# Two groups of attention matmuls a step instead of four in a fused attention and MoE kernel

## The chip, the core and the metric

The kernel runs on one core of a Trainium2 chip. The metric is the time of one execution in device microseconds: the median of three runs before the change is 851.68 us (850.89 to 852.7). Traces and pages come from one profiled execution. Engines are named as the profile names them: PE (TensorE) with its weight loads PEld, DVE (VectorE), ACT (ScalarE), POOL (GpSimd) and SP (SyncE, which issues all DMAs here; its queue is SPq).

## What is computed

Attention for 8 batches of 8 heads with 512 local and 32 global tokens of 64 values: global tokens attend to all, local tokens to the global ones and to a window of 32 to each side. Its output, 4608 tokens of 512 values, goes through a layer that takes the largest of three products and multiplies it by a fourth matrix.

```python
    s_g = scale * np.matmul(q_g, k_all.transpose(0, 1, 3, 2))
    out_g = np.matmul(sm(s_g), v_all)
    s_ll = scale * np.matmul(q_l, k_l.transpose(0, 1, 3, 2))
    mask = np.abs(pos[:, None] - pos[None, :]) <= window
    s_ll = np.where(mask, s_ll, -1000000000.0)
    s_lg = scale * np.matmul(q_l, k_g.transpose(0, 1, 3, 2))
    a_l = sm(np.concatenate([s_lg, s_ll], axis=-1))
    out_l = np.matmul(a_l, np.concatenate([v_g, v_l], axis=2))
...
    h = np.maximum(np.maximum(x @ w1, x @ w2), x @ w3)
    return (h @ w_out).astype(np.float32)
```

Everything is in 32-bit floats. From tile 28 on the attention's operands, and in the MoE layer all of them, are split in a high part and a rest, so that a product is made of two or three matmuls.

## The kernel before

**Tiles and steps.** Two heads make a pair `p`; a batch has four pairs, and a pair four tiles of 128 local queries. There are 128 tiles `sl`, with `t = sl % 4`. The main loop makes one step for each tile (lines 510 to 539). A step works on several tiles at once, since each is at another stage: it transposes the probabilities of tile `sl + 1` (`trans`, four matmuls into the PSUM tile `T`, read by a copy and, from tile 26 on, a subtraction into `pt`), computes the scores of tile `sl + 3` (`next_scores` calls `scores`; PSUM tile `S`), and multiplies tile `sl`'s probabilities with the values (`pv`, PSUM tile `O`). For the next pair's global tokens, `glob` makes scores in the steps with `t` 0 and 1 (PSUM tile `S` again) and `glob_soft` their softmax in the step with `t` 2; six small DMAs (line 298) bring it into `probg`. `transg` transposes one block of `probg` for tile `sl + 1` (one matmul, PSUM tile `S`), and its copy completes `pt`.

**The way of the local scores.** VectorE reads the score tile with the mask and finds the extreme value (line 325), ScalarE takes the exponential and its sum (line 327), VectorE the reciprocal (lines 329 and 330), some engine multiplies by it (`times`, mostly POOL at line 112), and SP issues the DMA into one of two `prob` tiles (line 334). Two steps later `trans` reads it.

**The MoE layer in the gaps.** From tile 16 on the previous batch's MoE layer runs between these pieces. `moe_group` is a generator that issues one wide matmul (512 columns) each time it is asked: 216 at line 425 (PSUM tile `pm`, three buffers) and 72 at line 444. `fill(n)` asks for `n`. A step asks for 4 + 4 + 3 + 7 = 18, so that 16 steps make the 288 of one batch. The last batch and the global tokens' MoE layer come after the loop.

**Buffers.** The tiles named `S` share two PSUM buffers, `T` and `O` have one each.

**Order.** TensorE keeps the program's order but for a few places. On all engines a scheduler in the framework orders the instructions when the program is built, and the functions `copy`, `sub` and `times` give work to the engine with the least load by their own planned costs; each engine then runs its own list in order and waits at its head.

**Weights.** Up to tile 25 the steps also convert the MoE weights (`weight_step`): a DMA into `wraw` (line 160), an absolute value on ScalarE (165), four bit operations on VectorE (168 to 171), a copy on ScalarE (178) and a subtraction on POOL (182).

## Time and profile before

| | before |
|---|---|
| median of three runs | 851.68 us (850.89 to 852.7) |
| the profiled execution | 852.36 us |
| its span, first to last instruction | 850.6 us |
| mean granted TensorE clock | 0.981 |
| first step of the changed kind (tile 16) begins | about 79 us |
| last attention matmul | about 744 us |

A line of the page names the source line, the engine, the operation and its tiles as out<-in; a timeline row has the start, the time from the first instruction's start to the last one's end, and the instructions that were merged (x4). The time of a busy matmul in such a row overlaps with the next one's, so that distances between starts are the better measure; the chain's pieces are made of these. A bracket is idle time of the engine ahead of the instruction, with what ended it. A row by stretches has the length, each engine's busy time with its instructions, the granted clock, the DMA share and GB/s.

### The profile page before, as it was taken

To read this page: it belongs to the slowest core of one execution; us is meant where nothing else is said; L and a number is where in the kernel's file an instruction comes from. 1 tells how busy PE (TensorE), PEld (TensorE's weight loads), DVE (VectorE), ACT (ScalarE), POOL (GpSimd) and SP (SyncE) were. 2 spreads that over 40 slices of the span, in tenths; PEclk is the share of its full clock that TensorE was granted. 3 is DMA by queue.
4 is the path that set the end of the run, shared out by engine and by line. 5 is a ranking of instruction groups with operands and counts; after the bars stand their busy time and mean duration, and the time that the engine had idled before them with its cause. 6 is when DMAs were issued, how large, how long until landed. Compare 5 with 4: busy or idle time off the path is not lost.

```text
span 850.6 us, 15712 instructions
## 1 busy us (share of the span) xinstructions
PE 811.6 (95%) x4452; PEld 674.6 (79%) x4452; DVE 566.0 (67%) x1784; ACT 527.9 (62%) x1479; POOL 510.0 (60%) x683
## 2 busy tenths in 40 slices
PE   6767987999999999999999999999999999999997
PEld 4545666788888888888888888888888888888896
DVE  4768786776777777777777777867786776421111
ACT  5666556767767676766776777776776676411111
POOL 5645666786668666766768766866676664411211
PEclk9798989999999999999999999999999999999999
DMA  6655755434333533353333433253335322100000
GB/s 199 173 175 159 223 168 161 125 109 136 111 108 89 155 101 104 105 163 113 95 107 114 136 110 102 85 161 106 98 113 162 101 85 67 65 12 1 25 25 25
DMA packets 102886, 95.12 MB, mean 112 GB/s; under 512 B 20752, under 2 KB 93584, under 8 KB 102800
## 3 DMA queue, kind: packets, MB, share of 16 engines
q1 hardware_dynamic: 102800, 94.12, 36.3%
q8 instruction: 36, 0.59, 0.3%
q14 instruction: 50, 0.41, 0.2%
HBM read 56.85 MB, written 8.91 MB: 77 GB/s over the span
## 4 chain that ended last, share of the span: by engine, by line
PE 87%; DVE 5%; DMA 2%; issue 2%; ACT 2%; SPq 1%; POOL 0%; DVEq 0%; ACTq 0%; POOLq 0%
PE pm L425 48%; PE pm L444 17%; PE O L394 7%; PE S L322 5%; PE T L346 4%; PE S L277 2%; PE O L387 1%; DVE wraw L170 1%; DMA wraw<-w_in 1%; PE S L367 1%; PE pm L318 1%; PE S L318 1%; DVE cut L169 1%; DVE cut L168 1%; PE S L273 0%
## 5 line engine op out<-in xcount | busy, mean ns | idle before, releaser
L425 PE MATMUL pm<-xs,wh 128*128 128x512 f32 (+1 forms) x1296 | 409.4, 389 | 0.8 <-POOL xs L94 0.8
L425 PEld LDWEIGHTS pm<-xs,wh 128*128 128x128 f32 x1296 | 234.2, 190 | 32.8 <-POOL xs L94 1.2
L425 PE MATMUL pm<-xs,wl 128*128 128x512 f32 (+1 forms) x648 | 254.1, 392 | 0.0
L112 POOL TENSOR_SCALAR s<-s,z 128x192 f32<-128x192 f32 (+1 forms) x220 | 101.6, 474 | 67.0 <-ACT lox L102 36.5
L425 PEld LDWEIGHTS pm<-xs,wl 128*128 128x128 f32 x648 | 123.0, 190 | 23.5 <-issue 2.4
L444 PE MATMUL pm<-woh,h 128*128 128x512 f32 x408 | 133.4, 398 | 0.0
L94 POOL TENSOR_TENSOR h<-m,h 128x512 fp32r<-128x512 f32 (+1 forms) x54 | 67.9, 1258 | 99.6 <-ACT h L102 99.6
L433 DVE TENSOR_TENSOR m<-pm,m 128x512 f32<-128x512 f32 (+1 forms) x108 | 71.2, 659 | 72.6 <-PE pm L425 71.6
L327 ACT ACTIVATE s<-s,nm 128x192 f32<-128x192 f32 (+1 forms) x224 | 103.1, 461 | 9.1 <-DVE nm L325 6.9
L94 POOL TENSOR_TENSOR qs<-qraw,qs 128x256 fp32r<-128x256 f32 x100 | 73.9, 749 | 57.4 <-ACT qs L102 44.0
L94 DVE TENSOR_TENSOR pt<-T,pt 128x512 fp32r<-128x512 f32 x102 | 70.5, 691 | 46.4 <-ACT pt L102 44.7
L329 DVE TENSOR_SCALAR z<-z 128x2 f32<-128x2 f32 x128 | 54.9, 429 | 48.7 <-ACT s L327 47.6
L444 PEld LDWEIGHTS pm<-woh,h 128*128 128x128 f32 x408 | 74.6, 188 | 11.6
L325 DVE CUSTOM_DVE_ANT_0 s<-S,mask 128x192 f32<-128x192 f32 (+1 forms) x224 | 74.7, 371 | 12.0 <-PE S L318 5.5
L444 PE MATMUL pm<-wol,h 128*128 128x512 f32 x204 | 81.7, 401 | 0.0
L94 POOL TENSOR_TENSOR vs<-vraw,vs 128x256 fp32r<-128x256 f32 x102 | 75.2, 737 | 7.7 <-ACT vs L102 3.6
L94 POOL TENSOR_TENSOR kst<-kraw,kst 64x576 fp32r<-64x576 f32 x49 | 70.1, 1430 | 11.4 <-issue 6.9
L102 ACT CAST pt<-T 128x512 fp32r<-128x512 f32 x90 | 52.7, 586 | 38.3 <-PE T L346 38.3
L102 ACT CAST qs<-qraw 128x256 fp32r<-128x256 f32 x100 | 40.7, 407 | 56.1 <-PE S L322 55.1
L394 PEld LDWEIGHTS O<-pt,vs 128*128 128x128 f32 x408 | 66.4, 188 | 9.2
L394 PE MATMUL O<-pt,vs 128*128 128x320 f32 (+1 forms) x408 | 72.8, 299 | 0.0
L346 PEld LDWEIGHTS T<-identr,prob 128*128 128x128 f32 x448 | 50.8, 141 | 20.6 <-ACT xr L102 2.3
(100 smaller groups left out, 1312.4 us busy)
## 6 DMA issues: line engine op xcount, KB each, us to landing
vraw<-v_in SPq DMA_DIRECT2D x128, 128.0 KB, 2.3
qraw<-q_in SPq DMA_DIRECT2D x100, 128.0 KB, 2.2
prob<-s SPq DMA_DIRECT2D x56, 224.0 KB, 2.4
prob<-s SPq DMA_DIRECT2D x56, 192.0 KB, 2.3
wraw<-w_in SPq DMA_DIRECT2D x18, 512.0 KB, 4.8
out_dram<-o SPq DMA_DIRECT2D x32, 256.0 KB, 2.5
kraw<-k_in SPq DMA_DIRECT2D x25, 320.0 KB, 3.1
qn<-q_in SPq DMA_DIRECT2D x28, 128.0 KB, 2.8
```

The source lines that it names most:

```text
L94: (dve if least(c) == "d" else pool).tensor_tensor(out=out, in0=a, in1=b, op=ALU.subtract)
L102: act.copy(out=out, in_=a)
L112: pool.tensor_scalar(out=out, in0=a, scalar1=col, scalar2=1.0, op0=ALU.mult, op1=ALU.mult)
L322: pe.matmul(ph[j][:, 0:n], lhsT=qs[sl][:, a, 128 * j:128 * j + 128], rhs=kst[p][:, j, c0:c0 + n], start=(a == 0), stop=(a == 1))
L325: dve.tensor_tensor_reduce(out=s[:, j, 0:n], in0=ph[j][:, 0:n], in1=mask[:, (1, 0, 1, 0)[t], 32 * (t == 0):32 * (t == 0) + n], scale=-0.12 ...
L327: act.activation(out=s[:, j, 0:n], in_=s[:, j, 0:n], func=AF.Exp, bias=nm[:, j:j + 1], scale=-1.0, accum_out=z[:, j:j + 1])
L329: dve.tensor_scalar(out=z, in0=z, scalar1=1e-9, scalar2=None, op0=ALU.add)
L346: i = pe.transpose(pr[:, 256 * j + 128 * c:256 * j + 128 * c + 128], s[:, j, 128 * c:128 * c + 128], one)
L394: pe.matmul(o[:, j, 0:320].rearrange("p (a q) -> p a q", a=2)[:, :, 0:n], lhsT=vs[sl][:, 2 * j + c].rearrange("p a d -> p (a d)"), rhs=pt[ ...
L425: pe.matmul(ps[:, 0:n], lhsT=w[f][:, i, k], rhs=xs[k][:, a, 0:n], start=(q == 0), stop=(q == 11))
L433: dve.tensor_tensor(out=m[:, 0:n], in0=ps[:, 0:n], in1=m[:, 0:n], op=ALU.max)
L444: pe.matmul(ps, lhsT=hh[f][:, a, 128 * t:128 * t + 128], rhs=w[:, f], start=(q == 0), stop=(q == 17))
```

## The change

```diff
@@ -514,21 +514,30 @@
+        steady = sl >= EARLY
         trans(sl + 1)
-        fill(4)
+        if not steady:
+            fill(4)
         next_scores(max(min(sl + 5, EARLY - 1), sl + 3))
         if t == 2:
             split_k(p + 2)
             load_k(p + 3)
-        fill(4)
+        if steady:
+            fill(8)
+            transg(sl + 1)
+        else:
+            fill(4)
         pv(sl)
         if t <= 1:
             glob(p + 1, t)
         elif t == 2:
             glob_soft(p + 1)
-        fill(3)
-        transg(sl + 1)
-        fill(7)
+        if steady:
+            fill(10)
+        else:
+            fill(3)
+            transg(sl + 1)
+            fill(7)
```

`EARLY` is 16. From step 16 on the transposes are followed at once by the scores, then come 8 wide matmuls, then the global transpose, the value products and the global scores together, then 10 wide matmuls. No instruction of TensorE is added or removed.

TensorE in a steady step with global scores (`t` 1, in the middle of the program), before; T is the transposes, S<-kst,qs the scores, O the value products, S<-kst,qgz the global scores:

```order
L346 MATMUL T<-identr,prob_92 128x128 x4
L425 MATMUL pm<-xs,wh_105 128x512 x2
L425 MATMUL pm<-xs,wl_111 128x512
L425 MATMUL pm<-xs,wh_105 128x512
L322 MATMUL S<-kst,qs 128x192 x4
L425 MATMUL pm<-xs,wh_105 128x512
L425 MATMUL pm<-xs,wl_111 128x512
L425 MATMUL pm<-xs,wh_105 128x512 x2
L394 MATMUL O<-pt,vs 128x320 x4
L277 MATMUL S<-kst,qgz 128x160 x2
L425 MATMUL pm<-xs,wl_111 128x512
L425 MATMUL pm<-xs,wh_105 128x512 x2
```

The global transpose (L367) follows, and 7 wide matmuls. The same step of the changed kernel, TensorE again:

```order
L346 MATMUL T<-identr,prob_92 128x128 x4
L322 MATMUL S<-kst,qs 128x192 x4
L425 MATMUL pm<-xs,wh_105 128x512 x2
L425 MATMUL pm<-xs,wl_111 128x512
L425 MATMUL pm<-xs,wh_105 128x512 x2
L425 MATMUL pm<-xs,wl_111 128x512
L425 MATMUL pm<-xs,wh_105 128x512 x2
L367 MATMUL S<-identr,probg_95 128x128
L394 MATMUL O<-pt,vs 128x320 x4
L277 MATMUL S<-kst,qgz 128x160 x2
```

Ten wide matmuls follow. The scores moved up to the transposes, and the global transpose moved ahead of the value products. In two steps, 19 and 23, the scheduler leaves the global transpose behind the value products, 3 and 10 wide matmuls later.

ScalarE around step 22, where it meets the fourth conversion of a `wo` weight (L165 wct), before; sg is the global scores:

```order
L290 ACTIVATE sg,zg<-sg,nmg 64x544
L178 CAST woh<-wct 128x512
L327 ACTIVATE s,z<-s,nm 128x224
L165 ACTIVATE wct<-wraw 128x512
L327 ACTIVATE s,z<-s,nm 128x224
L102 COPY xr<-O 128x160
L110 ACTIVATE sg<-sg,zg 64x544
```

ScalarE at the same place after the change:

```order
L178 CAST woh<-wct 128x512
L327 ACTIVATE s,z<-s,nm 128x224 x2
L165 ACTIVATE wct<-wraw 128x512
L102 COPY pt<-S 128x2x2x32
L102 COPY xr<-O 128x160
L290 ACTIVATE sg,zg<-sg,nmg 64x544
```

Both exponentials of the local scores now stand ahead of the weight's absolute value, and the exponential of the global scores behind it; their scaling (L110 before) went to POOL.

SP's DMAs ahead of the global transpose of step 23, before:

```order
L160 DMA wraw<-wo_in 128x512
L253 DMA vraw<-v_in 128x256
L298 DMA probg_94<-sg 64x128
L298 DMA probg_94<-sg 64x96
L160 DMA wraw<-wo_in 128x512
L334 DMA prob_93<-s 128x2x224
L298 DMA probg_94<-sg 64x96
L298 DMA probg_94<-sg 64x64
L298 DMA probg_94<-sg 64x96
L298 DMA probg_94<-sg 64x64
```

SP there after the change:

```order
L160 DMA wraw<-wo_in 128x512
L241 DMA qraw<-q_in 128x256
L253 DMA vraw<-v_in 128x256
L334 DMA prob_93<-s 128x2x224
L160 DMA wraw<-wo_in 128x512
L298 DMA probg_94<-sg 64x128
L298 DMA probg_94<-sg 64x96 x2
L298 DMA probg_94<-sg 64x64
L298 DMA probg_94<-sg 64x96
L298 DMA probg_94<-sg 64x64
```

All six transfers of the global tile moved behind the `prob` transfer of the local scores and behind a weight's load.

## The prediction

> **What bounds the kernel now.** I read the page first, then the busy time by stretches, then the chain that ended last.

> ```profile
> span 850.6 us, 15712 instructions
> PE 811.6 (95%) x4452; PEld 674.6 (79%) x4452; DVE 566.0 (67%) x1784; ACT 527.9 (62%) x1479; POOL 510.0 (60%) x683
> PE 87%; DVE 5%; DMA 2%; issue 2%; ACT 2%; SPq 1%; POOL 0%; DVEq 0%; ACTq 0%; POOLq 0%
> 300.00:400.00 100.00, 100.00 (x555) 84.89 (x554) 74.74 (x243) 71.68 (x204) 68.88 (x96) 1.00 0.38 116
> 108.50:115.33 6.83, 5.05 (x15) 0.50 0.57 150
> 146.05:149.46 3.41, 3.41 (x11) 0.50 0.62 202
> ```

> TensorE is busy 95% of the span and carries 87% of the chain. From 300 to 400 us it is busy for all 100 us at a granted clock of 1.00, so that there no other engine ends a wait: a gain must be TensorE's own time. Only the stretch up to about 150 us is different: in the last two rows (which list TensorE alone) the granted clock is 0.50 for 6.83 and 3.41 us. The change acts from 79 us on, so it meets some 70 us of the second kind and about 660 us of the first.

> One steady step, as the chain has it in order of time (start, duration, instructions; T is the transposes, S the scores, O the value products, L277 the global scores, L367 the global transpose, pm the wide MoE matmuls):

> ```profile
> 408.10 0.29 PE T L346 x4
> 408.39 1.00 PE pm L425 x4
> 409.39 0.42 PE S L322 x4
> 409.81 0.95 PE pm L425 x4
> 410.76 0.58 PE O L394 x4
> 411.34 0.19 PE S L277 x2
> 411.53 0.73 PE pm L425 x3
> 412.26 0.06 PE S L367
> 412.32 1.67 PE pm L425 x7
> ```

> Every matmul brings its own weight load. This is the load row of the neighbouring step (start and duration; one of 0.64 us holds four):

> ```profile
> 402.58 0.19 PEld L425 LDWEIGHTS pm<-xs,wl 128*128 128x128 f32 x1
> 402.81 0.19 PEld L425 LDWEIGHTS pm<-xs,wh 128*128 128x128 f32 x1
> 403.05 0.64 PEld L322 LDWEIGHTS S<-kst,qs 128*128 128x128 f32 x4
> 403.60 0.19 PEld L425 LDWEIGHTS pm<-xs,wh 128*128 128x128 f32 x1
> 403.71 0.19 PEld L425 LDWEIGHTS pm<-xs,wl 128*128 128x128 f32 x1
> 406.20 0.19 PEld L425 LDWEIGHTS pm<-xs,wl 128*128 128x128 f32 x1
> 406.31 0.42 PEld L425 LDWEIGHTS pm<-xs,wh 128*128 128x128 f32 x2
> ```

> Between wide matmuls loads start 0.23 us apart (402.58, 402.81): one wide matmul takes that long and hides the next load. After the narrow scores (403.60 to 403.71) and after the global transpose (406.20 to 406.31) the next one starts 0.11 us later. I read 0.11 us as the time of a load that nothing hides: a matmul keeps TensorE for its own stream or for the load of its successor, whichever is longer.

> **The change, part by part.** It moves instructions and changes no count: each step keeps 18 wide matmuls, 4 T, 4 S, 4 O, at most 2 global scores and 1 global transpose.

> *Junctions on TensorE.* The wide matmuls take 4 x 0.23 = 0.92 of the 1.00 us behind T, so 0.08 us is extra; behind the global transpose it is 1.67 - 7 x 0.23 = 0.06 us. If a load that finds no cover is the reason, then the extra belongs to the narrow matmul ahead, not to the return to wide ones. In the new order the last transpose is followed by a score, whose load takes 0.11 us as well (403.05 is such a group), and the global transpose by a value product, whose load has the same 128x128 form. The first score and the first value product lose the wide matmul that hid their load, and two wide matmuls get a wide neighbour: as many loads are bare as before. I take 0.0 us for 112 steps. The lower bound, were both extras the price of a switch, is -(0.08 + 0.06) x 112 = -15.7 us. The upper bound is an instruction that waits for semaphores, which would no longer run beside a wide matmul; the group of the global transpose has it at 51 ns:

> ```profile
> L367 PEldq EVENT_SEMAPHORE  x96: 51/51/4514, 18.9 to 736.6; - x96
> ```

> Two per step give 2 x 0.051 x 112 = +11.4 us. I stay at 0.0, since 0.051 fits beside a bare load of 0.11.

> [...]

> *Waits in a steady step.* These rows are of the timeline, with the start first: a step with global scores, and the step that reads a new global tile.

> ```profile
> 407.94 0.45 PE L346 MATMUL T<-identr,prob 128*128 128x128 f32 x4
> 410.14 0.35 DVE L325 CUSTOM_DVE_ANT_0 s<-S,mask 128x192 f32<-128x192 f32 x1
> 415.86 3.70 SPq L298 DMA_DIRECT2D probg<-sg  x6
> 419.42 0.46 PE L346 MATMUL T<-identr,prob 128*128 128x128 f32 x4
> 423.36 0.22 PE L367 MATMUL S<-identr,probg 128*128 128x128 f32 x1
> probg<-sg SPq DMA_DIRECT2D x96, 24.0 KB, 1.9
> ```

> The three tiles named S share two buffers. In the old order the global transpose waited for the scores' buffer; in the new one the global scores do, right behind the value products. VectorE has read the scores at 410.14 + 0.35 = 410.49, 2.55 us after T began. It reads T's copy first, so earlier scores hardly move that. The global scores now begin 0.29 + 0.06 + 0.42 + 0.03 + 8 x 0.23 + 0.11 + 0.58 = 3.33 us after T (pieces as above). About 0.8 us is left, and behind such a wait the whole TensorE queue would stand. The other wait is the global transpose of the step that needs the six probg transfers: the last issue begins near 415.86 + 3.70 - 0.60 = 418.96 and lands 1.9 us later, at 420.9; before, the transpose came at 423.36, now near 419.42 + 2.7 = 422.1. The reserve falls from 2.5 to 1.2 us. The next T's `prob`, by contrast, gains about 1 us, since the scores come before the wide matmuls. Both reserves stay positive: 0.0 us.

> *The stretch from 79 to 150 us.* Here weights are still converted, and TensorE waits twice for probg:

> ```profile
> 110.28 0.34 PE L367 MATMUL S<-identr,probg 128*128 128x128 f32 x1 [4.47 <-DMA probg<-sg]
> 123.96 1.70 POOL L112 TENSOR_SCALAR s<-s,z 128x192 f32<-128x192 f32 x2
> 128.75 2.40 POOL L112 TENSOR_SCALAR s<-s,z 128x192 f32<-128x192 f32 x2 [1.29 <-ACT wct L165]
> 131.17 0.60 SPq L334 DMA_DIRECT2D prob<-s  x1
> 132.75 0.39 SPq L160 DMA_DIRECT2D wraw<-wo_in  x1
> 136.37 0.67 ACT L165 ACTIVATE wct<-wraw 128x512 f32<-128x512 f32 x1 [2.22 <-DMA wraw<-wo_in]
> 136.94 0.47 ACT L327 ACTIVATE s<-s,nm 128x224 f32<-128x224 f32 x1
> 140.21 0.64 SPq L334 DMA_DIRECT2D prob<-s  x1
> 140.90 2.58 SPq L298 DMA_DIRECT2D probg<-sg  x4
> 144.70 0.25 PE L367 MATMUL S<-identr,probg 128*128 128x128 f32 x1 [3.14 <-issue]
> ```

> At 110.28 the global transpose keeps its place behind the value products and 11 wide matmuls, and SP's order just ahead of its transfers is unchanged: 0.0 us. At 144.70 it is different. Before, ScalarE's second exponential (136.94) stood behind a weight's absolute value that waited for its DMA (136.37); SP's `prob` (140.21) and four probg transfers followed. Now both exponentials stand ahead of that wait, but the exponential of sg behind it, and all six transfers go out after `prob` and a weight load. From the same landing at 136.37, sg's exponential ends about 138.3; VectorE's conversion steps ahead of its reciprocal end near 139.7; the scaling on POOL ends near 140.5; the sixth issue begins 3.1 us later and lands 1.8 us after that, at 145.4: +0.7 us. Against it, the weight's transfer (132.75) stands on SP behind `prob` (131.17), and that behind a scaling that took 2.40 us where the same pair took 1.70 at 123.96; with that and the earlier scores I put it out some 1.4 us sooner. The sum is -0.7 us. The bounds: the wait of 3.14 us goes, and with it half of the 3.41 us at clock 0.50, -4.8 us; or it grows by the 0.7 us and a second stretch at half clock follows (1.7 us) at each of the two waits, +4.1 us.

> [...]

> **Sum.** The profiled execution took 852.36 us, 1.8 us around its span of 850.6, and lies 0.68 us above the median of 851.68. 852.36 + 0.0 + 0.0 - 0.7 = 851.7, and 851.0 by the median's measure.

> **Rivals.**
> 1. *A switch has a price of its own* and two of them go: 851.7 - 15.7 = 836.0 us. For it: the time behind T and the global transpose is longer. Against it: the load rows explain this without a switch. 8%.
> 2. *The second early wait dissolves*, with its half clock: 851.7 - 4.8 = 846.9 us. For it: everything before it moves earlier. Against it: sg's chain now stands behind the weight's wait. 12%.
> 3. *The global scores wait for the scores' buffer* (slower). It decides once VectorE reads the scores later than 3.3 us after T. At 0.1 us over, in the two of four steps that have them, 56 x 0.1 = +5.6: 857.3 us. Against it: 0.8 us of reserve. 12%.
> 4. *The early waits grow* and pull the clock down for one more stretch each: 851.7 + 4.1 = 855.8 us. The order of ScalarE and SP has changed in both directions there. 13%.

> That the change doesn't do what it says holds for two of 112 steps only, where the global transpose stays behind the value products; it is in the forecast.

> **How the numbers follow.** The forecast has 55%, within 849 and 854. 0.2% is 1.7 us, about what a measurement can tell from no change. Of the 55, 12 are faster by more than that (the early wait shortens by over 1.7 us), 43 within it. Faster: 12 + 12 + 8 = 32%. Same: 43%. Slower: 12 + 13 = 25%. The range goes from the second rival, 846.5, to the fourth, 856.0; it leaves out the first and most of the third.

> **What would show it.** In the new trace four T and four S should stand together at about 0.79 us, the global transpose, O and global scores together at about 0.9; wide matmuls inside a run keep 0.23 us; steps keep 5.9, 5.6 and 5.7 us; no wait shows after 170 us. Steps shorter by 0.1 us would prove the switch's price; idle time ahead of L277 would be rival 3. The idle rows at about 110 and 145 us, and the stretches at 0.50, decide the early term. Wrong would be above all that one bare load costs the same whatever follows.

## The result, and the profile after

The change made the kernel slower: the median is 858.1 us (four runs, 856.79 to 859.05) against 851.28 us of before, measured beside it (four runs, 850.39 to 852.7). The ratio is 1.0077, with a 95% interval of 1.0056 to 1.0099. The profiled execution took 859.05 us.

The page of after, its first line, the engines and the chain's shares:

```profile
span 857.2 us, 15705 instructions
PE 813.7 (95%) x4452; PEld 678.7 (79%) x4452; DVE 561.3 (65%) x1785; ACT 519.5 (61%) x1479; POOL 509.8 (59%) x682
PE 81%; DVE 8%; DMA 4%; ACT 3%; issue 2%; POOL 0%; SPq 0%; DVEq 0%; ACTq 0%; POOLq 0%
```

The span grew by 6.6 us and TensorE's busy time by 2.1. In the chain TensorE fell from 87% to 81% and VectorE rose from 5% to 8%: somewhere TensorE now waits for VectorE. The steady part isn't the place. The chain of after in the step that the prediction dissected (start, duration, instructions):

```profile
415.18 0.30 PE T L346 x4
415.48 0.49 PE S L322 x4
415.97 1.87 PE pm L425 x8
417.85 0.06 PE S L367
417.90 0.64 PE O L394 x4
418.54 0.19 PE S L277 x2
418.73 2.33 PE pm L425 x10
```

The extra that stood behind T is gone (8 wide matmuls take 1.87 us, or 0.23 each), and the scores carry it instead (0.49 us where they took 0.42). The step lasts 421.06 - 415.18 = 5.88 us by the next step's start, and lasted 5.89.

The next table sets the starts of the first transposes of all steps side by side. It is worked out from those rows; a step is numbered by its tile `sl`.

| stretch | before, us | after, us | difference |
|---|---|---|---|
| first transposes to step 25 | 139.83 | 139.98 | +0.15 |
| step 25 | 6.25 | 9.44 | +3.19 |
| steps 26 to 28 | 17.23 | 17.31 | +0.08 |
| step 29 | 5.97 | 9.54 | +3.57 |
| step 30 to the last transposes | 553.89 | 553.57 | -0.32 |

Two steps hold the whole loss. The list of TensorE's waits between 150 and 740 us (in total, times, longest) names them; the trace of before has no wait of TensorE after 160 us:

```profile
PE S L322 <- DVE pt L94: 1.9, 1, 1.9
PE S L277 <- DVE nm L325: 1.9, 1, 1.9
PE T L346 <- DMA prob<-s: 0.6, 3, 0.2
```

**Step 25** in the timeline of after: TensorE's rows, then VectorE's, then one of POOL (start, length, and in brackets the idle time ahead):

```profile
153.37 0.46 PE L346 MATMUL T<-identr,prob 128*128 128x128 f32 x4
153.67 0.66 PE L322 MATMUL S<-kst,qs 128*128 128x192 f32 x4
158.81 0.45 PE L277 MATMUL S<-kst,qgz 128*128 128x160 f32 x2 [1.86 <-DVE nm L325]
...
153.25 0.50 DVE L168 TENSOR_SCALAR wct<-wct 128x512 f32<-128x512 f32 x1 [0.84 <-ACT wct L165]
153.78 1.53 DVE L169 TENSOR_SCALAR wct<-wct 128x512 int32<-128x512 int32 x1
155.35 1.11 DVE L170 SCALAR_TENSOR_TENSOR wraw<-wraw,wct 128x512 int32<-128x512 int32 x1
156.50 1.10 DVE L171 SCALAR_TENSOR_TENSOR wct<-wraw 128x512 int32<-128x512 int32 x1
157.52 0.68 DVE L94 TENSOR_TENSOR pt<-T,pt 128x512 fp32r<-128x512 f32 x1
158.39 0.35 DVE L325 CUSTOM_DVE_ANT_0 s<-S,mask 128x192 f32<-128x192 f32 x1
...
153.54 1.49 POOL L94 TENSOR_TENSOR kst<-kraw,kst 64x576 fp32r<-64x576 f32 x1
```

The global scores take the buffer that the same step's local scores used, and VectorE reads those only when it has converted the last piece of weights: its second read ends at 158.39 + 0.35 = 158.74, 5.4 us after T began, not 2.55. The rows of before at the same place show how near the edge this step already was:

```profile
153.71 0.43 DVE L169 TENSOR_SCALAR wct<-wct 128x512 int32<-128x512 int32 x1
157.22 0.35 DVE L325 CUSTOM_DVE_ANT_0 s<-S,mask 128x192 f32<-128x192 f32 x1
157.64 0.28 PE L367 MATMUL S<-identr,probg 128*128 128x128 f32 x1
```

There the reads ended at 157.57, and the global transpose, which then needed that buffer, began at 157.64: a reserve of 0.07 us. The same 0.07 us lie between the read and the matmul that did wait for it (158.74 and 158.81), so that nothing was to spare. In the new order the global scores were due at 158.81 - 1.86 = 156.95, 3.58 us after T. In before, where T began at 153.19, the reads ended 4.38 us after T, so that 0.80 us would be missing even against VectorE's old times. The other 0.99 us came from VectorE being later, about as much as line 169 alone is longer (1.53 us for 0.43). In after the planner (the functions `copy`, `sub` and `times`, which choose an engine) gave a subtraction of `kst` to POOL, which ran beside it, where before VectorE had done it ahead (0.95 us at 152.15).

**Step 29** is a sister of it, between other tiles:

```profile
182.45 0.69 PE L322 MATMUL S<-kst,qs 128*128 128x192 f32 x4 [1.87 <-DVE pt L94]
...
177.34 1.54 DVE L100 CAST kst<-kraw 64x576 fp32r<-64x576 f32 x1
178.91 1.80 DVE L94 TENSOR_TENSOR xs<-xr,xs 128x512 fp32r<-128x512 f32 x1
180.64 1.37 DVE L329 TENSOR_SCALAR z<-z 128x2 f32<-128x2 f32 x1
182.12 0.27 DVE L94 TENSOR_TENSOR pt<-S,pt 128x128 fp32r<-128x128 f32 x1
```

The local scores, now right behind T, need the buffer of the previous step's global transpose. Its last reader (the row at 182.12) stands behind a copy of `kst`, a subtraction of `split_x` and a small operation on `z`. That subtraction is the only one of `split_x` on VectorE in the whole trace; before has none. Without its 1.80 us the read would end at 180.59, and the scores were due at 180.58. Here too the trace of before had nothing to spare: the local scores began at 177.97, and VectorE's read of the global scores, whose buffer they then took, ended at 177.33 + 0.55 = 177.88.

**The clock** accounts for the rest. The row by stretches lists TensorE's busy time and the granted clock; each pair is the stretch of 3.41 us that holds the wait, and the next one:

```profile
156.43:159.84 3.41, 1.55 (x14) 1.00 0.39 116
159.84:163.25 3.41, 3.41 (x12) 0.50 0.49 143
180.32:183.73 3.41, 1.54 (x12) 1.00 0.00 0
183.73:187.15 3.42, 3.42 (x12) 0.50 0.67 217
```

By the granted clock, a stretch at 0.50 that matmuls fill costs half of 3.41, or 1.71 us. In the timeline seven wide matmuls take the 2.97 us from 159.84 to 162.81, or 0.42 us each for 0.23 at full clock, which gives 1.54 us. With a wait of 1.87 that is 3.6 or 3.4 us for each place, an estimate, against +3.19 and +3.57 measured. The first half-clock stretch ends at 163.25, and so 0.44 us of it lie in step 26.

The early waits that the prediction treated by themselves hardly moved (4.47 and 3.14 us before):

```profile
109.51 0.37 PE L367 MATMUL S<-identr,probg 128*128 128x128 f32 x1 [4.41 <-DMA probg<-sg]
145.20 0.25 PE L367 MATMUL S<-identr,probg 128*128 128x128 f32 x1 [3.46 <-DMA probg<-sg]
```

### The profile page after: what moved, and what is told of

Its sections match the earlier page's. It is cut to its first block, busy times and chain, and to the rows that moved or that the text cites. A ratio compares the mean times of both kernels' runs of the same rounds, so it can differ in the third digit from the quotient of the medians.

```text
span 857.2 us, 15705 instructions
## 1 busy us (share of the span) xinstructions
PE 813.7 (95%) x4452; PEld 678.7 (79%) x4452; DVE 561.3 (65%) x1785; ACT 519.5 (61%) x1479; POOL 509.8 (59%) x682
## 4 chain that ended last, share of the span: by engine, by line
PE 81%; DVE 8%; DMA 4%; ACT 3%; issue 2%; POOL 0%; SPq 0%; DVEq 0%; ACTq 0%; POOLq 0%
PE pm L425 45%; PE pm L444 15%; PE O L394 7%; PE S L322 6%; PE T L346 4%; DVE wraw L170 2%; DMA wraw<-w_in 2%; PE S L277 1%; PE O L387 1%; PE pm L318 1%; PE S L367 1%; DMA wraw<-wo_in 1%; DMA prob<-s 1%; DVE z L329 1%; ACT s L327 1%
## 5 line engine op out<-in xcount | busy, mean ns | idle before, releaser
L425 PE MATMUL pm<-xs,wh 128*128 128x512 f32 (+1 forms) x1296 | 389.7, 384 | 0.0
L425 PEld LDWEIGHTS pm<-xs,wh 128*128 128x128 f32 x1296 | 235.6, 191 | 38.0 <-issue 0.2
L425 PE MATMUL pm<-xs,wl 128*128 128x512 f32 (+1 forms) x648 | 249.6, 385 | 0.0
L112 POOL TENSOR_SCALAR s<-s,z 128x192 f32<-128x192 f32 (+1 forms) x218 | 99.9, 470 | 95.8 <-ACT pt L102 51.2
L425 PEld LDWEIGHTS pm<-xs,wl 128*128 128x128 f32 x648 | 123.1, 190 | 23.4 <-issue 2.4
L327 ACT ACTIVATE s<-s,nm 128x192 f32<-128x192 f32 (+1 forms) x224 | 103.3, 462 | 49.2 <-DVE nm L325 48.6
L444 PE MATMUL pm<-woh,h 128*128 128x512 f32 x408 | 128.1, 395 | 0.0
L329 DVE TENSOR_SCALAR z<-z 128x2 f32<-128x2 f32 x128 | 64.9, 507 | 52.4 <-ACT s L327 50.0
L394 PE MATMUL O<-pt,vs 128*128 128x320 f32 (+1 forms) x408 | 78.8, 315 | 0.0
L325 DVE CUSTOM_DVE_ANT_0 s<-S,mask 128x192 f32<-128x192 f32 (+1 forms) x224 | 73.6, 365 | 3.1 <-PE S L318 3.1
L94 POOL TENSOR_TENSOR kst<-kraw,kst 64x576 fp32r<-64x576 f32 x50 | 71.9, 1438 | 6.0 <-ACT kst L102 1.2
L322 PE MATMUL S<-kst,qs 128*128 128x192 f32 (+1 forms) x400 | 66.5, 288 | 1.9 <-DVE pt L94 1.9
L346 PEld LDWEIGHTS T<-identr,prob 128*128 128x128 f32 x448 | 50.8, 142 | 20.9 <-issue 3.0
L394 PEld LDWEIGHTS O<-pt,vs 128*128 128x128 f32 x408 | 59.3, 190 | 9.4 <-issue 0.2
```

The source lines that it names most:

```text
L94: (dve if least(c) == "d" else pool).tensor_tensor(out=out, in0=a, in1=b, op=ALU.subtract)
L112: pool.tensor_scalar(out=out, in0=a, scalar1=col, scalar2=1.0, op0=ALU.mult, op1=ALU.mult)
L322: pe.matmul(ph[j][:, 0:n], lhsT=qs[sl][:, a, 128 * j:128 * j + 128], rhs=kst[p][:, j, c0:c0 + n], start=(a == 0), stop=(a == 1))
L325: dve.tensor_tensor_reduce(out=s[:, j, 0:n], in0=ph[j][:, 0:n], in1=mask[:, (1, 0, 1, 0)[t], 32 * (t == 0):32 * (t == 0) + n], scale=-0.12 ...
L327: act.activation(out=s[:, j, 0:n], in_=s[:, j, 0:n], func=AF.Exp, bias=nm[:, j:j + 1], scale=-1.0, accum_out=z[:, j:j + 1])
L329: dve.tensor_scalar(out=z, in0=z, scalar1=1e-9, scalar2=None, op0=ALU.add)
```

## The experiments

The theory: the groups cost nothing in themselves; two buffer waits in steps 25 and 29, where VectorE is late, and the half clock behind them are the whole loss. The main rivals: the groups cost a little in every step; or VectorE's lateness costs the same whichever instruction meets it.

### 1. Groups from step 32 on

```diff
-        steady = sl >= EARLY
+        steady = sl >= 32
```

> The groups are made from step 32 on; steps 16 to 31 keep the order of before. Theory (the loss is two waits of 1.9 us in steps 25 and 29, each with 3.41 us of half clock behind it; later steps are 0.015 us shorter each): both waits are gone, 96 steps give 96 x 0.015 = 1.4, so 849.9 us (849 to 851.5). Rival (the groups cost a little in every step): 96 of 112 steps keep their share of the 6.8 us, so 857 us.

Measured: ratio 0.9997 (0.9984 to 1.0011), a median of 852.01 us beside 852.76 of before. The two waits are gone; the longest left is 0.7 us, for a `prob` transfer. So 96 grouped steps cost nothing, and the first rival falls. The 1.4 us that I hoped for from them don't show either.

### 2. Only steps 25 and 28 as before

```diff
-        steady = sl >= EARLY
+        steady = sl >= EARLY and sl not in (25, 28)
```

> Only steps 25 and 28 go back to the order of before, the other 110 stay grouped; step 28 because its global transpose is in the buffer for which the scores of step 29 wait. Theory (two buffer waits): both go, 850 to 852 us. Rival (VectorE is late there whatever the order, and another TensorE instruction waits in place of these two): 854 to 858 us, with a new wait of TensorE over 1 us between 153 and 190 us.

Measured: ratio 1.0047 (1.0027 to 1.0066). The rival was nearer. TensorE's and VectorE's rows of this kernel:

```profile
158.78 0.28 PE L367 MATMUL S<-identr,probg 128*128 128x128 f32 x1 [0.81 <-DVE nm L325]
180.48 0.69 PE L322 MATMUL S<-kst,qs 128*128 128x192 f32 x4 [1.62 <-DVE nmg L281]
179.87 0.55 DVE L281 CUSTOM_DVE_ANT_0 sg<-S,sg 64x384 f32<-64x384 f32 x1
```

In step 25 the old order puts the global transpose behind the late read, with 0.81 us of wait. In step 28, where the `split_x` subtraction is on VectorE here too, the old order hardly helped: with the global transpose last, the scores of step 29 get the buffer of the global scores, which VectorE reads at 179.87, and they wait 1.62 us where after has 1.87. Neither wait has half clock behind it; the two steps last 7.24 and 7.68 us. Who waits is decided by the ring of the two buffers, not by one step alone.

### 3. The global scores in another buffer

```diff
-        ps = psS.tile([128, 512], F32, name="S")
+        ps = pm.tile([128, 512], F32, name="pm") if p > 4 else psS.tile([128, 512], F32, name="S")
```

> All 112 steps stay grouped and each engine keeps its order; from the fifth pair on the global scores go to a buffer of the wide matmuls (pm) instead of one of the two S buffers. Theory (the wait is for the S buffer, not for VectorE's time as such): no wait of the global scores near 157 us and none of the local scores near 182 us, 850 us (849 to 852). Rival 1 (VectorE's lateness costs the same elsewhere): 854 to 858. Rival 2 (three pm buffers become too few, wide matmuls wait in each of 56 steps): over 858.

Measured: ratio 1.0019 (1.0001 to 1.0037). Step 25 is right: it takes 6.16 us and has no wait. Step 29 is half right, at 7.36 us; the waits from 153 to 205 us in this kernel are:

```profile
PE O L394 <- DVE xr L402: 0.9, 1, 0.9
PE T L346 <- DMA prob<-s: 0.4, 1, 0.4
PE S L367 <- DVE pt L94: 0.2, 1, 0.2
```

The buffer of the value products is met instead. In step 28 VectorE is so late that the shared buffer was only the first thing in its way, as the rival said, though for less time. Three `pm` buffers remain enough.

### 4. One subtraction moved to GpSimd

```diff
-        sub(d[1], src, f32(d[0]))
+        if forced:
+            spend("p", n * 2.32 + 130)
+            pool.tensor_tensor(out=d[1], in0=src, in1=f32(d[0]), op=ALU.subtract)
+        else:
+            sub(d[1], src, f32(d[0]))
...
-            xs.setdefault(b, []).append(split_x(xr[q][:, :, 0:128], SL))
+            xs.setdefault(b, []).append(split_x(xr[q][:, :, 0:128], SL, b == 1))
```

> As after, but the subtraction of split_x that the planner had given to VectorE in step 28 (1.80 us at 178.91) is forced to GpSimd. Theory: only the second wait (1.87 us at 182.45) goes or falls under 0.2 us, with the half clock behind it; the first stays: 858.1 - 1.8 - 1.7 = 854.6 us (853.8 to 855.4). Rival 1 (the half clock comes whatever the wait): only the wait goes, 856.3 us. Rival 2 (the late VectorE work isn't what holds the buffer): 858 us, wait unchanged.

Measured: ratio 1.0063 (1.0045 to 1.0082), a median of 857.14 us. That is more than expected and nearer to the first rival's 856.3 (1.0059 of the 851.28 of before beside the result), though in the profiled execution the second wait is gone: step 29 takes 6.48 us. Smaller waits for a `prob` transfer (0.4 us) and for POOL (0.2 us) came. The first wait is there, in the timeline of this kernel:

```profile
159.63 0.46 PE L277 MATMUL S<-kst,qgz 128*128 128x160 f32 x2 [2.09 <-DVE nm L325]
```

The stretch that holds most of it and the next one, with TensorE's busy time and the granted clock, show another side of the clock:

```profile
155.90:159.31 3.41, 1.64 (x13) 1.00 0.31 85
159.31:162.72 3.41, 3.09 (x18) 1.00 0.34 97
```

A wait of 2.09 us, longer than those of after, and no half clock behind it: step 25 takes 8.28 us, the 6.25 of before and the wait. The grid of 3.41 us on which the clock changes (last section) lies so in this execution, by the rows above, that 1.77 us of the wait fall in one window and the rest in the next. The half clock isn't a fixed price of a wait.

### 5. VectorE relieved at both places

TensorE's order is that of after. The last weight piece's four operations are queued behind step 25's score reads, the last calls of `weight_step` move from steps 23 to 25 to steps 25 to 27 (`WS`), and the subtraction goes to GpSimd as in experiment 4 (`last[0]` is the second score read traced last; the other three operations stand in the same block):

```diff
-        dve.tensor_scalar(out=f32(c), in0=f32(c), scalar1=2.0 ** -15, scalar2=HIMAX, op0=ALU.max, op1=ALU.min)
+        with tc.issue_after(last[0]) if m == 23 else ExitStack():
+            dve.tensor_scalar(out=f32(c), in0=f32(c), scalar1=2.0 ** -15, scalar2=HIMAX, op0=ALU.max, op1=ALU.min)
...
-    WS = [0, 0, 0, 1, 0, 1, 0, 1, 0, 1, 0, 1, 2, 2, 1, 2, 2, 1, 2, 2, 1, 2, 2, 1, 2, 2]
+    WS = [0, 0, 0, 1, 0, 1, 0, 1, 0, 1, 0, 1, 2, 2, 1, 2, 2, 1, 2, 2, 1, 2, 2, 0, 0, 1, 1, 1]
```

> TensorE's order is that of after. VectorE alone is relieved at the two places: the last weight piece's four bit operations are queued behind step 25's score reads instead of ahead of them, and split_x's subtraction goes to GpSimd as in the fourth experiment. Theory (the groups cost only where VectorE reads the scores' buffers too late): both waits are under 0.3 us, 1.000 of before (0.998 to 1.002). Rival 1 (the order itself needs VectorE earlier in more than these places, new waits come): 1.004 or more. Rival 2 (the groups gain once the waits are gone): under 0.998.

Measured: ratio 1.0009 (0.9993 to 1.0025). All of TensorE's waits from 153 to 740 us, with line numbers some lines further down in this kernel:

```profile
PE T L349 <- DMA prob<-s: 0.8, 3, 0.3
PE pm L451 <- POOL h L94: 0.3, 1, 0.3
```

The same order of TensorE that loses 0.8% in after loses nothing here. The loss is VectorE's lateness at two places, and the groups themselves are neutral; the rival of a hidden gain falls too.

### 6. The first place alone

The edit of experiment 5 without the forced subtraction.

> As the fifth, but only the last weight piece is moved behind step 25's score reads; the rest stays as in after. Theory: the wait of the global scores in step 25 (1.86 us) goes; the second stays if VectorE's late work in step 28 still stands there, and the time is before plus 1.9 to 3.6 us, ratio 1.002 to 1.0045. If the planner's later choices put the subtraction of split_x elsewhere by themselves, the second wait goes too and the ratio is 1.000. Rival (a wait of the same length comes elsewhere in step 25): 1.006 or more.

Measured: ratio 1.0012 (0.9995 to 1.0029); neither wait is left (the longest is 0.7 us, for POOL). The planner by itself gave no subtraction of `split_x` to VectorE this time, the branch that the expectation left open. It doesn't separate the two places, but it shows that a small edit elsewhere makes or removes the second stall.

### 7. The scores alone moved up

```diff
-        if steady:
-            fill(8)
-            transg(sl + 1)
-        else:
-            fill(4)
+        fill(8 if steady else 4)
         pv(sl)
...
-        if steady:
-            fill(10)
-        else:
-            fill(3)
-            transg(sl + 1)
-            fill(7)
+        fill(3)
+        transg(sl + 1)
+        fill(7)
```

> From step 16 on only the scores move up to the transposes; the global transpose stays behind the value products and three wide matmuls, as before. Theory (either half needs VectorE earlier: local scores 0.9 us earlier than before, global scores no longer behind the same step's score reads): no wait of the global scores in step 25, one of up to 1 us of the global transpose for the score reads there, and one of 1 to 1.6 us of the local scores in step 29; no half clock behind these, ratio 1.003 (1.001 to 1.005). Rival (all of the loss comes from moving the global transpose ahead): 1.000, no wait over 0.3 us.

Measured: ratio 1.0134 (1.0109 to 1.0159), far outside what I expected. From 205 to 740 us:

```profile
PE S L322 <- DVE nmg L281: 7.8, 21, 0.8
```

Half of the change is worse than the whole. With the global transpose left behind, the local scores of each step with `t` = 1 get the buffer of the previous step's global scores, as in before, but are due 1 us sooner. By the starts of the transposes those steps from 33 on last 6.42 us on the mean for 5.89, 0.53 x 23 = 12 us. The list shows less, since idle time counts only from the end of the transposes' row, which overlaps with the next matmul. Moving the global transpose between scores and global scores hands the local scores another buffer; that is why the whole change is free in a steady step. On steps 25 and 29 this run says little: the planner left the `split_x` subtraction to POOL and no `kst` subtraction runs beside line 169 (0.43 us), and of the waits expected there only 0.6 us for the local scores came.

### 8. Control: the relief in the kernel before

The edit of experiment 6 (that of experiment 5 without the forced subtraction) on the kernel of before, where the planner already has that subtraction on POOL.

> Control: TensorE's order of before, with the last weight piece's bit operations queued behind step 25's score reads as in the fifth. Theory (before waits nowhere there, so that relief brings it nothing): 1.000 (0.998 to 1.002). Rival (the relief is a gain in itself, and hides a cost of the groups in the fifth): under 0.998.

Measured: ratio 1.0001 (0.9989 to 1.0014). The relief is no gain in itself.

### 9. The changed kernel again

> The changed kernel once more, unaltered, for the price of its two waits. Theory (a wait of about 1.9 us always comes, and the half clock of 3.41 us behind it only where about 1.7 us or more of the wait lie in one window of a grid of 3.41 us that runs on by itself): both waits are there again, 1.5 to 2.2 us each; behind each the clock is half or full according to the grid of that execution, so that the times spread from before + 3.2 to before + 7.2 us, ratio 1.004 to 1.0085. Rival (each such wait is followed by half clock always): both are, and the times lie together at 1.0075 to 1.0085.

Measured: ratio 1.0085 (1.006 to 1.011), four runs from 855.2 to 860.9 us. Both waits came, 2.73 and 1.86 us, each with half clock behind it. This does not decide between theory and rival; the spread of 5.7 us is larger than either expected.

### 10. Groups in steps 16 to 31 only

```diff
-        steady = sl >= EARLY
+        steady = EARLY <= sl < 32
```

> The groups are made in steps 16 to 31 only, and from step 32 on the order is that of before: the complement of the first experiment. Theory (all of the loss lies in steps 25 and 29, and the other 110 steps are neither shorter nor longer): both waits are there, ratio as in the run of after beside it, 1.004 to 1.0085. Rival (the grouped steps from 32 on lose time too, or gain it): the ratio differs from that of after by 0.003 or more.

Measured: ratio 1.0087 (1.0055 to 1.0119), that of experiment 9 beside it. All of the loss lies in these 16 steps. The waits are 1.89 and 1.88 us, and the windows around them:

```profile
155.96:159.37 3.41, 1.61 (x8) 1.00 0.53 150
159.37:162.78 3.41, 3.41 (x15) 0.50 0.54 148
179.85:183.26 3.41, 1.80 (x10) 1.00 0.09 27
183.26:186.67 3.41, 3.41 (x20) 1.00 0.64 214
```

The same wait, once with half clock behind it and once without: in the second a part of the idle time (1.61 of 1.88 us) lies in the window. Step 29 takes 7.94 us there, not 9.54. With experiment 4 this shows that the rival of experiment 9 is wrong.

## Why the prediction was wrong

- **Junctions on TensorE (0.0): right.** The chain's rows give 0.79 us for T and S together, as foretold, and 0.89 us for global transpose, O and global scores, for 0.9. The extra moved from T to the scores, as it should if it is the price of a bare load; that cause wasn't tried by itself. Experiments 1 and 5 confirm the 0.0 at 0.9997 and 1.0009.
- **Waits in a steady step (0.0): the failed step.** "Both reserves stay positive" was worked out from one step near 410 us and applied to all 112. In that step it holds: the reads end 2.34 us after T and the global scores begin at 3.36, for the 2.55 and 3.33 of the prediction. From step 32 on all that is left are three waits of 0.2 us for `prob`, a transfer that the prediction saw gain 1 us. In steps 25 and 29 VectorE still converts weights or splits `xs` beside `kst` for the first time, and there the first reserve does not hold (5.37 us after T in step 25), nor does one that the prediction didn't list (step 29): the term is 2 x 3.4 us, not 0. The prediction's claim that no wait shows after 170 us fell with it. The reserve of 0.07 us at 157.64 stood in the trace of before.
- **The early stretch (-0.7): not shown.** The two waits are 4.41 and 3.46 us, together 0.26 us longer, and the way to step 25 took 0.15 us more. In experiment 9 the same kernel needed 4.1 us less for it than in the first execution, so a single trace cannot decide a term of that size. One more stretch at half clock for each was my estimate and didn't come: after has 6.83 us (from 108.64 on) and 3.41 us (from 146.19 on) at 0.50 there, as before has. The second wait of before, 3.14 us, is shorter than a window of 3.41 us: the one from 142.64 to 146.05 us held 1.35 us of matmuls and was followed by 3.41 us at 0.50. So half clock also came behind a window that matmuls partly filled, and this price was missing from the third rival.
- **Rival 3 had the mechanism** in step 25: the global scores wait for the scores' buffer. Its price was of the wrong kind: I spread 0.1 us over 56 steps, where one step paid 1.86 us of wait and, by the estimate above, 1.5 to 1.7 us of clock. The second stall is a sister that I had not listed, local scores behind the global transpose's buffer. And the edit also changed whom the planner gives work: a `kst` subtraction to POOL beside line 169, and a `split_x` subtraction to VectorE. The prediction followed such shifts only up to 150 us.
- **The upper bound of 856.0** left out most of that rival, so the time fell outside the range.

Experiment 5 shows that late VectorE work at these two places is the cause; that line 169's extra 1.10 us is due to POOL's neighbour is read from traces (it recurs in four more, see the last section) and wasn't tried by itself.

## What to carry to other kernels

A reserve ahead of a shared buffer has to be read in the worst step, not in a steady one: list for each phase when the last reader of a buffer ends and when its next writer is due. Moving one instruction between two users of a ring of buffers changes who inherits which buffer, so the order of all its users counts, and half a change can cost more than the whole. On TensorE, which bounds this kernel, a short wait was paid nearly twice where half clock came behind it (1.87 us of wait and an estimated 1.5 to 1.7 us of clock).

## What the runs showed of the hardware

```profile
137.95:141.36 3.41, 1.57 (x7) 1.00 0.53 178
141.36:144.77 3.41, 2.62 (x16) 1.00 0.42 123
```

- A VectorE operation of 0.43 us took 1.53 us beside a POOL subtraction of 1.49 us (line 169, above) and ended 0.28 us after it. In the traces of experiments 2, 3, 4 and 10 the same row takes 1.54 us beside the same subtraction and ends 0.28 or 0.29 us after it; in those of before and of experiments 1 and 7, where that subtraction doesn't run beside it, it takes 0.43 to 0.53. A small operation (line 329) takes up to 0.20 us in 66 of the 128 steps of after and over 1 us in 19; its 1.37 us in step 28 lie beside two POOL subtractions of `kst`. No run here changes that subtraction alone.
